# One Exp over four PSUM banks, and a planned fill of the attention steps, in a fused attention and GEGLU kernel

## The chip, the cores and the metric

The kernel runs on one core of one Trainium2 chip. The metric is the device time of one execution in microseconds (us); each kernel is run several times, and the median is compared. TensorE is called PE below, VectorE DVE, ScalarE ACT, GpSimd POOL, and SyncE SP, as the profile has them.

## The reference

One layer norm feeds two branches whose results are added to the input. S = 2048 positions, D = 448 features, H = 16 heads of 28, a sliding window of 256 positions, and F = 1792 hidden features, all bf16.

```python
xn = (x - mean(x)) / sqrt(var(x) + 1e-5)
q, k, v = split(xn @ wqkv)                      # 16 heads of 28
scores = q @ k.T * 28 ** -0.5
mask   = (i - j >= 0) & (i - j < 256)           # causal, 256 wide
a = softmax(where(mask, scores, -1e9)) @ v      # heads joined again
b = (gelu_tanh(xn @ w_gate) * (xn @ w_up)) @ w_down
out = x + a @ wo + b
```

## The kernel before

**Blocks and stages.** The positions are cut into four blocks of 512 (`qb` 0 to 3), each of four tiles of 128. Each block has an attention stage and then a gate stage. Each engine executes its instructions in the order in which the Python code issues them; the order is written out by hand, and engines wait for each other through semaphores.

**Attention stage** (`attention`). The 16 heads are taken in 4 groups of 4 (`g`), and each group in 3 steps (`n`), since a block of 512 queries and its window are cut into three pieces of at most 512 score columns a head. So a block has 12 steps, called steps 0 to 11 here. In a step PE computes the scores `sc` of four heads (keys on the partitions) into four PSUM banks, ACT turns them into `p_sb` with Exp (no maximum is subtracted; a guard at the end checks the sums and branches to a general path that does not run here), and POOL zeroes what lies outside the window (`affine_select`). In the second step of the next group PE multiplies `p_sb` with `v_sb` into `ov` (`pv`); `v_sb` has a column of ones, so that the sums of the softmax come out as one row of `ov`. `ov` is copied to `oc`, the "inverse" chain on DVE (two 32x32 transposes, a small copy, a reciprocal) turns the sums into the factors `rb`, and POOL multiplies `oc` by them into `oN`.

**Fillers.** PE needs other work while ACT does the Exp. Generators deliver it in pieces: `gen_proj` (transposes `tp`, and the projections `pv`, `pq`, `pk` to V, Q and K of the next block), `gen_up` (up projections `ue` done early), and `gen_down` (the output tiles `po` of the block before: 4 matmuls with `wo` on `oN`, 14 with `wd` on `hT`, then DVE adds the input into `res`, and SP stores it). A `Feed` wraps a generator with its estimated time left, and `share` decides after each step's Exp which feed delivers how much; a step that has stopped at `HOLD` does its last matmuls (contraction over the last 64 features, split tiles, "halves") and its copies at the start of the next step. Estimates are in ns of PE time.

**Gate stage** (`gated`). For pairs of 128 hidden features PE computes `gt` and `u`, ACT applies gelu (`ge`), DVE multiplies into `hT`. Gelu and Exp need different ACT tables, so each change of stage loads one. The function `hook` puts statistics of later tiles (`stat`) behind some pairs.

**PSUM.** There are 8 banks: tag `s` 2 x 2 banks (scores, or `gt`), tag `m` two banks, tags `d` and `o` one each. `ov` takes `d` while the current output tile `po` has `o`, and the other way round; `bank` hands out `m` (and `d` in block 0) to the projections in turn.

**Layer norm.** `stat` (DVE), `rstd` (two small ACT operations) and `norm` (DVE) of a tile; before, the four tiles of a later block are scaled in one piece (`prep`) at the beginning of an attention stage, and those of block 1 in the first two steps of block 0.

Of the kernel before, what the change touches and what calls it, by code (L numbers as in the profile page):

```python
# [9 lines left out]
ALU = mybir.AluOpType  # L10
# [6 lines left out]
P = 128  # L17
# [7 lines left out]
HOLD = None  # L25


class Feed:
# [10 lines left out]
    def run(self):  # L39
        self.held = False  # L40
        while self.gens:
# [5 lines left out]
            if c is HOLD:  # L47
                self.held = True
                return 0
# [18 lines left out]


@with_exitstack  # L70
def kernel(
# [18 lines left out]

    xv = A_x.rearrange("b (n p) d -> p (b n) d", p=P)
# [22 lines left out]
    for a in range(2):  # L114
        nc.sync.dma_start(out=wraw[64 * a:64 * a + 64, 3, 0:D], in_=A_wqkv[384:448, a * D:(a + 1) * D])
        nc.sync.dma_start(out=wv[64 * a:64 * a + 64, 3, :], in_=A_wqkv[384:448, 2 * D:3 * D])
# [6 lines left out]
    nc.gpsimd.memset(wo[:, :, :], 0.0)  # L123
# [6 lines left out]
    wo_v = A_wo.rearrange("(g j d) n -> j d g n", g=4, j=4)  # L130
    for j in range(4):
        nc.sync.dma_start(out=wo[32 * j:32 * j + Dh, :, :], in_=wo_v[j])
    nc.sync.dma_start(out=wd[:, :, :], in_=B_w_down.rearrange("(k p) n -> p k n", p=P))

# [20 lines left out]
    def warmup(n):  # L155
        for _ in range(n):
            wps = psum.tile([P, 2, QB], f32, name="wps", tag="s")
            nc.tensor.matmul(wps[:, 0, :], lhsT=warm[:, 0:P], rhs=warm[:, :], start=True, stop=True)
# [14 lines left out]
    def norm(t, eng):  # L173
        xn = work.tile([P, 4, P], bf16, name="xn", bufs=4)
        xf = xn[:, :, :].rearrange("p a b -> p (a b)")
        for lo, n, src in ((0, D, 0), (D, 64, 384)):
            eng.tensor_scalar(out=xf[:, lo:lo + n], in0=x_sb[:, t, src:src + n], scalar1=mv_all[:, t, 0:1],  # L177
                                    scalar2=rstd_all[:, t:t + 1], op0=ALU.subtract, op1=ALU.mult)
        xns[t] = xn

    def prep(qb):
        rstd(4 * qb, 4)
        for t in range(4 * qb, 4 * qb + 4):
            norm(t, nc.vector)
# [30 lines left out]
    def gen_v(qb, ts):  # L215

        for t in ts:
            pvs = []
            for i in range(2):
# [4 lines left out]
                yield 570  # L224
            yield HOLD
# [42 lines left out]
    def gen_down(qb, tags="odod"):  # L268

        hT, oN = hTs[qb], oNs[qb]  # L270
        for tt in range(4):
# [8 lines left out]
            for f in range(NF):  # L280
                nc.tensor.matmul(po[:, 0:D], lhsT=hT[:, f, cs], rhs=wd[:, f, :], start=False, stop=(f == NF - 1),  # L281
                                 skip_group_check=True)
                if f % 4 == 3:
                    yield 755
# [398 lines left out]
```

## Time and profile before

| | before |
|---|---|
| median of 3 runs | 247.76 us (247.2 to 248.15) |
| the profiled execution, its own time | 247.11 us |
| its span, first to last instruction | 245.4 us |
| PE busy | 228.6 us, 93% of the span |
| ACT busy | 141.3 us, 58% |
| DVE busy | 136.9 us, 56% |
| POOL busy | 96.3 us, 39% |
| mean granted PE clock | 0.989 of full speed |

All rows of the trace come from the one profiled execution; its span and its own time differ by what lies around the program. A row of a timeline gives start, length, engine, line, operation, tile written from tiles read, shape, and in brackets how long the engine stood idle before it and which instruction ended that. A row of a group gives busy time and mean ns of one, then idle time before and what ended it. Times of matmuls overlap, so that the distance between starts is the better measure of one.

### The profile page before, as it was taken

Reading aid. Unit: us, or ns where it says so; the run is one execution under the profiler, and the core shown is the slowest. Engines: PE = TensorE matmul, PEld = TensorE weight load, DVE = VectorE, ACT = ScalarE, POOL = GpSimd, SP = SyncE. Lnnn points to the kernel's source line nnn. Section 1 sums busy time; section 2 is a strip of 40 time slices with the busy share of each in tenths; the row PEclk is TensorE's granted clock in tenths of the full one; section 3 lists DMA queues with packets and bytes.
Section 4 is the critical chain, followed back from the end, with each engine's and each line's share of the span. In section 5 each row is a group of like instructions: output and inputs, shape, how many; then the busy total and the mean of one; then the engine's idle time right before and its main releaser. Section 6 shows DMA issues by size and latency. Waiting matters only on the chain.

```text
span 245.4 us, 4264 instructions
## 1 busy us (share of the span) xinstructions
PE 228.6 (93%) x1692; PEld 95.7 (39%) x1712; DVE 136.9 (56%) x272; ACT 141.3 (58%) x169; POOL 96.3 (39%) x120
## 2 busy tenths in 40 slices
PE   7887998999999999999999999999999889999990
PEld 2322432334354434444344334444443334344440
DVE  5977686756662664486663754573321564484311
ACT  3661667753687866633587867643378878645000
POOL 7223275522054865520045765620036677420000
PEclk9997999999999999999999999999999999999998
DMA  7999800000000000000000000000000000000010
GB/s 233 344 300 296 255 7 3 0 1 3 0 19 4 19 3 19 21 0 0 0 23 0 21 0 21 19 0 3 1 19 3 19 0 21 19 0 3 20 40 28
DMA packets 9010, 10.95 MB, mean 45 GB/s; under 512 B 600, under 2 KB 7960, under 8 KB 8984
## 3 DMA queue, kind: packets, MB, share of 16 engines
q1 hardware_dynamic: 8312, 9.69, 13.1%
q10 hardware_dynamic: 672, 0.92, 1.1%
q8 instruction: 15, 0.25, 0.4%
q14 instruction: 11, 0.09, 0.1%
HBM read 8.77 MB, written 1.84 MB: 43 GB/s over the span
## 4 chain that ended last, share of the span: by engine, by line
PE 80%; ACT 8%; DVE 7%; issue 1%; DMA 1%; ACTq 0%
PE po L281 16%; PE gt L197 15%; PE u L197 12%; ACT p_sb L445 7%; PE sc L440 6%; PE gt L202 5%; PE ov L414 5%; PE po L277 4%; PE pk L197 4%; PE pv L197 4%; PE pq L197 3%; PE ue L197 2%; PE pq L202 2%; DVE qT L247 2%; DVE xn L177 1%
## 5 line engine op out<-in xcount | busy, mean ns | idle before, releaser
L451 POOL TENSOR_SCALAR_AFFINE_SELECT p_sb<-p_sb 128x512 bf16<-128x512 bf16 (+1 forms) x92 | 69.5, 777 | 93.8 <-ACT p_sb L445 93.5
L445 ACT ACTIVATE p_sb<-sc 128x1024 bf16<-128x1024 f32 (+2 forms) x96 | 87.9, 969 | 24.5 <-PE sc L440 21.6
L281 PE MATMUL po<-wd,hT 128*128 128x448 bf16 x224 | 49.9, 354 | 0.0
L351 ACT ACTIVATE ge<-gt 128x1024 bf16<-128x1024 f32 x28 | 28.7, 1024 | 34.8 <-PE u L202 22.3
L355 DVE TENSOR_TENSOR hT<-ge,u 128x512 bf16<-128x512 bf16 x44 | 28.1, 679 | 29.4 <-ACT ge L351 29.4
L197 PE MATMUL gt<-xnT,wg 128*128 128x512 bf16 x161 | 39.8, 380 | 0.7 <-issue 0.5
L197 PE MATMUL u<-xnT,wu 128*128 128x512 bf16 x130 | 32.0, 379 | 0.1
L405 POOL TENSOR_TENSOR oN<-oc,rb 128x512 bf16<-128x512 f32 x16 | 20.9, 1305 | 24.6 <-DVE rb L399 24.6
L281 PEld LDWEIGHTS <-hT 128*128 128x128 bf16 x224 | 19.0, 98 | 20.9 <-issue 6.5
L440 PE MATMUL sc<-qT,kT 32*128 32x128 bf16 (+2 forms) x352 | 23.0, 279 | 3.0 <-ACT p_sb L445 2.5
L286 DVE TENSOR_TENSOR res<-po,x_sb 128x448 bf16<-128x448 f32 x16 | 9.7, 608 | 25.5 <-PE po L281 25.5
L197 PEld LDWEIGHTS <-wu 128*128 128x128 bf16 x168 | 16.1, 98 | 20.0 <-issue 1.6
L197 PEld LDWEIGHTS <-wg 128*128 128x128 bf16 x168 | 15.1, 98 | 22.0 <-issue 6.0
L247 DVE CAST qT<-pq 128x512 bf16<-128x512 f32 x16 | 10.9, 682 | 16.1 <-PE pk L202 16.0
L418 ACT COPY oc<-ov 128x512 f32<-128x512 f32 x16 | 9.4, 585 | 16.5 <-PE ov L414 15.3
L197 PE MATMUL pk<-xnT,wkp 128*128 128x512 bf16 x48 | 13.6, 394 | 2.7 <-DVE qT L247 2.7
L277 PE MATMUL po<-wo,oN 128*128 128x448 bf16 x64 | 14.7, 352 | 0.0
L440 PEld LDWEIGHTS <-kT 32*128 32x128 bf16 x352 | 7.6, 92 | 18.3 <-issue 17.3
L202 PE MATMUL gt<-xnT,wgu 64*128 64x512 bf16 x50 | 13.7, 379 | 0.0
L197 PE MATMUL pq<-xnT,wqp 128*128 128x512 bf16 x41 | 13.0, 394 | 0.5 <-issue 0.2
L316 DVE CAST hT<-ue 128x512 bf16<-128x512 f32 x12 | 7.7, 686 | 9.8 <-PE ue L202 9.8
L414 PE MATMUL ov<-p_sb,v_sb 128*32 128x128 bf16 (+2 forms) x352 | 12.8, 277 | 0.0
(65 smaller groups left out, 215.5 us busy)
## 6 DMA issues: line engine op xcount, KB each, us to landing
out_dram<-res SPq DMA_DIRECT2D x16, 112.0 KB, 1.7
wd<-in_B_w_down_dram SPq DMA_DIRECT2D x1, 1568.0 KB, 12.3
wu<-in_B_w_up_dram SPq DMA_DIRECT2D x1, 1344.0 KB
wg<-in_B_w_gate_dram SPq DMA_DIRECT2D x1, 1344.0 KB, 15.1
x_sb<-in_A_x_dram SPq DMA_DIRECT2D x1, 896.0 KB
wraw<-in_A_wqkv_dram ACTq DMA_DIRECT2D x1, 672.0 KB
x_sb<-in_A_x_dram SPq DMA_DIRECT2D x1, 448.0 KB
wo<-in_A_wo_dram SPq DMA_DIRECT2D x4, 98.0 KB
```

The lines of the kernel that those rows point to most:

```text
L197: nc.tensor.matmul(ps, lhsT=lhs(c), rhs=rhs(c), start=start and c == 0, stop=stop and c == 2, skip_group_check=True)
L202: nc.tensor.matmul(ps, lhsT=lhs[p0:p0 + 64], rhs=rhs[p0:p0 + 64], start=start, stop=stop, tile_position=(p0, 0), skip_group_check=True)
L247: nc.vector.tensor_copy(out=qT[:, g, ts], in_=pq[:, :])
L277: nc.tensor.matmul(po[:, 0:D], lhsT=oN[:, g, cs], rhs=wo[:, g, :], start=(g == 0), stop=False, skip_group_check=True)
L281: nc.tensor.matmul(po[:, 0:D], lhsT=hT[:, f, cs], rhs=wd[:, f, :], start=False, stop=(f == NF - 1), skip_group_check=True)
L351: nc.scalar.activation(out=ge[:, :, :], in_=pr["gt"][:, :, :], func=ACT.Gelu_apprx_tanh)
L355: nc.vector.tensor_tensor(out=hT[:, f + i, :], in0=ge[:, i, :], in1=u[:, :], op=ALU.mult)
L405: nc.gpsimd.tensor_tensor(out=oN[:, g, :], in0=oc[:, :], in1=rb[:, :, :].rearrange("p a b -> p (a b)"), op=ALU.mult)
L414: nc.tensor.matmul(ov[32 * j:32 * j + 32, q0:q0 + nq], lhsT=v_sb[:, kt, h, :], rhs=p_sb[:, j, col:col + nq], start=(n == 0 and i == 0), st ...
L440: nc.tensor.matmul(ss[j // 2][:, j % 2, col:col + nq], lhsT=kT[r, g, kt * P:(kt + 1) * P], rhs=qT[r, g, qb * QB + q0:qb * QB + q0 + nq], s ...
L445: nc.scalar.activation(out=p_sb[:, 2 * i:2 * i + 2, 0:ncol], in_=ss[i][:, :, 0:ncol], func=ACT.Exp, scale=SCALE)
L451: nc.gpsimd.affine_select(out=reg, in_=reg, pattern=mid + [[1 if diag else -1, P]], compare_op=ALU.is_ge, fill=0.0, base=0 if diag else -1 ...
```

## The change

- **One Exp a step.** The scores of a step go into one tile of four banks, and one ACT instruction reads them. The pool of that tile has one buffer in attention and is replaced by two buffers of two banks in the gate stage (`score_pool`).
- **`oc` is copied by DVE**, no longer by ACT.
- **`qT` in blocks 0 and 1 is copied by ACT** (`qb > 1` picks DVE), and one V copy more on ACT in block 1.
- **The fill is planned.** `share` gets amounts in ns for the two feeds: what remains, divided by the steps left, less what the step has anyway (`STEP` for scores, `PV` for `ov`), with the second feed's part from a table `plan`. `gen_down` delivers pieces of two matmuls. The last step takes all that is left.
- **Layer norm:** tiles of blocks 2 and 3 are scaled by `hook` in the gate stage before, one tile behind a pair; statistics of tiles 8 to 11 move into the steps of block 0.
- **Block 3** does five pairs' up projections in attention (`early`) instead of four.
- **Start:** the order of the first small weight loads, of two transposes' copies, of `wo`'s memset, and of one V projection.

```diff
-def share(feeds, parts):
-    want = [max(f.left, 0) / n if n else 1e12 for f, n in zip(feeds, parts)]
+def share(feeds, first, second):
+    want = [first, second]
     while True:
-        can = [i for i, f in enumerate(feeds) if f.gens and want[i] > 350 and (parts[i] == 0 or not f.held)]
+        can = [i for i, f in enumerate(feeds) if f.gens and want[i] > 190 and not f.held]
         if not can:
             return
-        i = max(can, key=lambda i: (not feeds[i].held, not feeds[i].closed, min(want[i], feeds[i].left)))
+        i = max(can, key=lambda i: (not feeds[i].closed, want[i]))
...
+def drain(feeds):
+    while any(f.gens for f in feeds):
+        min((f for f in feeds if f.gens), key=lambda f: (f.held, f.closed)).run()
...
+    phase = [None]
+    def score_pool(n):
+        if phase[0] is not None:
+            phase[0].close()
+        phase[0] = ExitStack()
+        phase[0].pool = phase[0].enter_context(tc.tile_pool(name="sps", bufs=n, space=bass.MemoryType.PSUM))
+    score_pool(1)
...
-            nc.vector.tensor_copy(out=qT[:, g, ts], in_=pq[:, :])
+            (nc.vector.tensor_copy if qb > 1 else nc.scalar.copy)(out=qT[:, g, ts], in_=pq[:, :])
             nc.vector.tensor_copy(out=kT[:, g, ts], in_=pk[:, :])
...
-            yield 760
+                if g % 2:
+                    yield 380
             for f in range(NF):
                 nc.tensor.matmul(po[:, 0:D], lhsT=hT[:, f, cs], rhs=wd[:, f, :], start=False, stop=(f == NF - 1),
                                 skip_group_check=True)
-                if f % 4 == 3:
-                    yield 755
+                if f % 2 and f < NF - 1:
+                    yield 375
...
-            nc.scalar.copy(out=oc[:, :], in_=ov[:, :])
+            nc.vector.tensor_copy(out=oc[:, :], in_=ov[:, :])
...
-                ss = [psum.tile([P, 2, QB], f32, name="sc", tag="s") for _ in range(2)]
+                ss = phase[0].pool.tile([P, 4, QB], f32, name="sc", tag="s")
...
-                for i in range(2):
-                    nc.scalar.activation(out=p_sb[:, 2 * i:2 * i + 2, 0:ncol], in_=ss[i][:, :, 0:ncol], func=ACT.Exp, scale=SCALE)
+                nc.scalar.activation(out=p_sb[:, :, 0:ncol], in_=ss[:, :, 0:ncol], func=ACT.Exp, scale=SCALE)
...
-                if qb and left > 10:
-                    share(feeds[:1], (left / 2,))
-                elif not qb and left > 1:
-                    while feeds[0].gens and not feeds[0].held:
-                        feeds[0].run()
-                elif left > 1:
-                    share(feeds, [left + 0.6] + [max(left - 1, 1)] * (len(feeds) - 1))
+                if left == 1:
+                    drain(feeds)
+                elif not qb:
+                    share(feeds + [Feed()], 1e12, 0)
                 else:
-                    share(feeds, [0] * len(feeds))
-                next(aux, None)
+                    to = plan.get(12 - left, 0)
+                    i = 12 - left
+                    whole = sum(f.left for f in feeds) + STEP * left + PV * sum(j > i for j in (4, 7, 10))
+                    ahead = STEP + (PV if n == 0 and g else 0) + (360 if to > 1000 else 0)
+                    share(feeds, whole / (left + 0.2) - ahead - to, to)
+                if aux:
+                    aux.pop(0)()
...
             if qb < 3:
                 feeds.append(Feed((gen_proj(qb + 1), PROJ)))
-                prep(qb + 1)
+                plan = {0: 830, 1: 830, 2: 1140, 4: 1140, 5: 1300, 7: 1300, 8: 1300, 10: 1300}
             else:
                 new_hT(3)
-                early = (2, 6, 8, 10)
+                early = (2, 4, 6, 8, 10)
...
-            elif f >= 4 and qb < 2 and f < 12:
-                stat(4 * qb + 8 + (f - 4) // 2)
+            elif f >= 4 and qb < 2:
+                t = 4 * qb + 4 + f // 2
+                if f < 12:
+                    norm(t + 2)
+                    if qb == 0:
+                        stat(t + 6)
```

The order that results, at the two places on which most hangs. First ACT, at the start of block 0's attention stage. Before, the Exps come in pairs and `lnv`, `rstd_all` (of block 1's layer norm) stand between them:

```order
L229 CAST v_sb<-pv 128x16x28 x3
L445 ACTIVATE p_sb<-sc 128x1024 x2
L168 ACTIVATE lnv<-mv_all,eps_t 128x4
L169 ACTIVATE rstd_all<-lnv 128x4
L445 ACTIVATE p_sb<-sc 128x2x384 x2
```

And after:

```order
L232 CAST v_sb<-pv 128x16x28 x2
L249 CAST qT<-pq 128x512
L447 ACTIVATE p_sb<-sc 128x2048
L177 ACTIVATE lnv<-mv_all,eps_t 128x4
L178 ACTIVATE rstd_all<-lnv 128x4
L249 CAST qT<-pq 128x512
L447 ACTIVATE p_sb<-sc 128x4x384
```

The copies of Q (`qT` from the bank `pq`) now stand on ACT between single Exps. In DVE's queue they stood behind the scaling of two tiles.

Second DVE, in block 3's attention stage, steps 5 and 6. Before (`ue` are the early up projections, `l` to `rb` the inverse chain, `res` a finished output tile):

```order
L316 CAST hT<-ue 128x512 x2
L394 STREAM_TRANSPOSE l_2382<-oc 128x512
L395 COPY l_all<-l_2382 128x16
L397 RECIPROCAL ri<-l_all 128x16
L399 STREAM_TRANSPOSE rb<-ri 128x512
L316 CAST hT<-ue 128x512 x2
```

And after:

```order
L319 CAST hT<-ue 128x512 x2
L397 STREAM_TRANSPOSE l_2316<-oc 128x512
L398 COPY l_all<-l_2316 128x16
L400 RECIPROCAL ri<-l_all 128x16
L402 STREAM_TRANSPOSE rb<-ri 128x512
L319 CAST hT<-ue 128x512 x2
L290 TENSOR_TENSOR res<-po,x_sb 128x448
L421 COPY oc<-ov 128x512
```

A `res` now stands behind the chain and the next two casts, and the copy of `ov`, that was ACT's, behind it. On PE, the rows just ahead of that `ov`, before:

```order
L281 LDWEIGHTS hT
L281 MATMUL po<-wd,hT 128x448
L414 LDWEIGHTS v_sb
L414 MATMUL ov<-p_sb,v_sb 32x128 [waits Pool_49]
L414 LDWEIGHTS v_sb
```

And after, where four matmuls with `wo` stand ahead and, before them, the two that end the tile of the `res` above:

```order
L280 LDWEIGHTS oN
L280 MATMUL po<-wo,oN 128x448
L417 LDWEIGHTS v_sb [waits DVE_49]
L417 MATMUL ov<-p_sb,v_sb 32x128 [waits Pool_49]
L417 LDWEIGHTS v_sb
```

`ov`'s first weight load waits for DVE now, as it did not before.

More of the change, by code (lines that the diff above doesn't have):

```diff
@@ L155, in warmup @@
     def warmup(n):
-        for _ in range(n):
-            wps = psum.tile([P, 2, QB], f32, name="wps", tag="s")
-            nc.tensor.matmul(wps[:, 0, :], lhsT=warm[:, 0:P], rhs=warm[:, :], start=True, stop=True)
+        wps = phase[0].pool.tile([P, 4, QB], f32, name="wps", tag="s")
+        for i in range(n):
+            nc.tensor.matmul(wps[:, i % 4, :], lhsT=warm[:, 0:P], rhs=warm[:, :], start=True, stop=True)
     def stat(t):
```

93 lines of the change are left out of this document (47 added, 46 removed).

## The prediction

> **What bounds the kernel now.** I read the page first, then the busy time per stage, then the timeline of TensorE around its gaps. The page has TensorE (PE) busy for 93% of the span:
>
> ```profile
> PE 228.6 (93%) x1692; PEld 95.7 (39%) x1712; DVE 136.9 (56%) x272; ACT 141.3 (58%) x169; POOL 96.3 (39%) x120
> ```
>
> The number of matmuls does not change, so the change can win only where PE stands still or runs at a lower clock. The four attention stages (blocks 0 to 3) by stage, with PE's busy time as the first number after the length and the granted clock (PEclk) after POOL:
>
> ```profile
> 14.20:46.00 31.80, 27.55 (x215) 10.21 (x216) 22.77 (x44) 19.26 (x29) 15.08 (x20) 0.95 0.52 142
> 66.60:98.90 32.30, 31.70 (x300) 14.10 (x302) 18.03 (x35) 24.56 (x30) 19.56 (x24) 1.00 0.04 12
> 122.50:154.80 32.30, 31.70 (x299) 14.08 (x301) 17.98 (x35) 24.56 (x30) 19.49 (x24) 1.00 0.04 12
> 178.50:208.50 30.00, 28.00 (x265) 11.83 (x269) 11.78 (x21) 24.11 (x27) 19.66 (x24) 1.00 0.04 13
> ```
>
> PE idles 4.25 us in block 0, 0.60 in blocks 1 and 2 each, 2.00 in block 3. Block 0 also loses clock, 0.05 of 31.8 us = 1.6 us. Its largest gap and what lies ahead of it on DVE:
>
> ```profile
> 17.02 0.82 PE L197 MATMUL pq<-xnT,wqp 128*128 128x512 bf16 x3
> 17.15 2.20 DVE L177 TENSOR_SCALAR xn<-x_sb,mv_all,rstd_all 128x448 bf16<-128x448 bf16 x4 [0.69 <-ACT rstd_all L169]
> 19.26 0.68 DVE L247 CAST qT<-pq 128x512 bf16<-128x512 f32 x1
> 19.99 0.81 PE L197 MATMUL pk<-xnT,wkp 128*128 128x512 bf16 x3 [2.15 <-DVE qT L247]
> 20.46 1.11 DVE L177 TENSOR_SCALAR xn<-x_sb,mv_all,rstd_all 128x448 bf16<-128x448 bf16 x4
> ...
> 22.00:23.00 1.00, 1.00 (x4) 0.41 (x3) 0.76 (x2) 0.46 (x1) 0.47 (x1) 0.50 1.05 326
> 25.00:26.00 1.00, 0.95 (x16) 0.77 (x14) 1.00 (x3) 1.00 (x2) 0.00 (x0) 1.00 1.16 256
> ```
>
> The `pk` matmul needs a PSUM bank that the copy `qT` empties, and DVE scales two tiles of the layer norm first. 1.5 us after that gap the clock is at half and PE is busy all the while.
>
> In blocks 1 to 3 the waits are for the Exp. A waiting step shows as two score matmuls, then the other six:
>
> ```profile
> 79.25 0.28 PE L440 MATMUL sc<-qT,kT 32*128 32x256 bf16 x2
> 79.95 0.39 PE L440 MATMUL sc<-qT,kT 32*128 32x256 bf16 x6 [0.42 <-ACT p_sb L445]
> 80.28 0.93 PE L281 MATMUL po<-wd,hT 128*128 128x448 bf16 x4
> ...
> 197.99 0.28 PE L440 MATMUL sc<-qT,kT 32*128 32x256 bf16 x2
> 198.91 0.39 PE L440 MATMUL sc<-qT,kT 32*128 32x256 bf16 x6 [0.63 <-ACT p_sb L445]
> 199.23 0.55 PE L281 MATMUL po<-wd,hT 128*128 128x448 bf16 x2
> ```
>
> Start to start such a step takes 1.03 and 1.24 us, where an unhindered one takes 0.33 (rows below), so 0.70 and 0.91 are lost where the view counts 0.42 and 0.63. Measured so over its 12 steps, block 1 loses 1.45 us, block 2 the same, block 3 3.05.
>
> **The change part by part.** Durations for the sums:
>
> ```profile
> L445 ACT ACTIVATE p_sb<-sc 128x1024 bf16<-128x1024 f32 x80 | 77.5, 1022 | 21.0 <-PE sc L440 18.2 <-POOL p_sb L451 2.7
> L445 ACT ACTIVATE p_sb<-sc 128x512 bf16<-128x512 f32 x8 | 4.3, 594 | 3.5 <-PE sc L440 3.4
> L418 ACT COPY oc<-ov 128x512 f32<-128x512 f32 x16 | 9.4, 585 | 16.5 <-PE ov L414 15.3 <-POOL p_sb L451 1.2
> L247 DVE CAST qT<-pq 128x512 bf16<-128x512 f32 x16 | 10.9, 682 | 16.1 <-PE pk L202 16.0
> L286 DVE TENSOR_TENSOR res<-po,x_sb 128x448 bf16<-128x448 f32 x16 | 9.7, 608 | 25.5 <-PE po L281 25.5
> ...
> 190.30 0.39 PE L202 MATMUL ue<-xnT,wug 64*128 64x512 bf16 x1
> 190.72 1.29 DVE L316 CAST hT<-ue 128x512 bf16<-128x512 f32 x2 [0.54 <-PE ue L202]
> 191.71 1.94 ACT L445 ACTIVATE p_sb<-sc 128x1024 bf16<-128x1024 f32 x2 [0.47 <-PE sc L440]
> 191.93 0.70 DVE L394 STREAM_TRANSPOSE l<-oc 128x512 f32<-128x512 f32 x1
> 193.48 0.71 DVE L399 STREAM_TRANSPOSE rb<-ri 128x512 f32<-128x512 f32 x1
> 193.70 0.39 PE L440 MATMUL sc<-qT,kT 32*128 32x128 bf16 x6 [0.34 <-ACT p_sb L445]
> 195.54 0.84 PE L414 MATMUL ov<-p_sb,v_sb 128*32 128x128 bf16 x24
> 196.31 0.40 PE L440 MATMUL sc<-qT,kT 32*128 32x384 bf16 x8
> 196.64 0.93 PE L281 MATMUL po<-wd,hT 128*128 128x448 bf16 x4
> 232.41 0.92 PE L277 MATMUL po<-wo,oN 128*128 128x448 bf16 x4
> 233.17 2.81 PE L281 MATMUL po<-wd,hT 128*128 128x448 bf16 x14
> 235.82 0.92 PE L277 MATMUL po<-wo,oN 128*128 128x448 bf16 x4
> ```
>
> *One Exp over four banks.* 512 more elements cost 428 ns, so 2048 take 1.022 + 2 x 0.428 = 1.88 us, against 1.94 for the pair: 0.07 less a step. The bounds are 1.88 and two that do not overlap, 2.04; I take 1.88, since the two sizes shown lie on its line. The price is that no score of the next step can start before the whole Exp has ended. A step then cannot be shorter than scores to Exp start (0.42), Exp 1.88, Exp end to scores 0.05: 2.35 us. Before, the limit was little different (Exp pairs at 191.71 and about 2.4 apart), plus 0.585 for the `oc` copy in every third step, which now leaves ACT.
>
> *Equal intervals.* The planned fill of each step in the new order, counted in matmuls: 0.19 us a down matmul (14 from 233.17 to 235.82), 0.77 a `ov` group (195.54 to 196.31), 0.33 the scores, and 0.1 where PE changes between full and split tiles. In blocks 1 and 2 steps 0 to 10 come to 2.3 to 2.8 us, in block 3 to 2.3 to 2.45. Nearly all lie at or just over 2.35. So the waits for the Exp go almost wholly; I leave 0.1 us in a block.
>
> *What is late next, first: step 0.* The table load behind the last gelu holds the first Exp, and the new order puts less work behind the first scores:
>
> ```profile
> 64.63 1.02 ACT L351 ACTIVATE ge<-gt 128x1024 bf16<-128x1024 f32 x1 [0.76 <-PE gt L197]
> 65.67 1.28 ACT L545 ACT_TABLE_LOAD   x1
> 67.41 1.92 ACT L445 ACTIVATE p_sb<-sc 128x1024 bf16<-128x1024 f32 x2
> 69.28 0.49 PE L440 MATMUL sc<-qT,kT 32*128 32x384 bf16 x8
> ```
>
> The Exp can start at the load's end, 66.95, and end at 68.85. Before, step 0 held scores and twelve `wd`, 2.7 us, so it began at 66.6; now it begins two `wo` (0.4) earlier, at 66.2, and holds scores, two `wo`, six `wd` and eight transposes (0.5), 2.4 us: PE is through at 68.6. So 0.3 us is lost in each of blocks 1 to 3, where nothing was lost.
>
> *Second: the attention output by DVE, and `ov`'s bank.* The copy costs DVE between 0.585 and 0.70 us (L418 on ACT, L394 on DVE), I take 0.68 (L247); 16 of them are 10.9 us more for DVE, 9.4 less for ACT. DVE has room on average (18.0 of 32.3 us busy in block 1, 11.8 of 30.0 in block 3) but not in bursts. `ov` takes the bank that `po` of the finished tile held, so its weight load waits until DVE has done `res` (the order shows a wait for DVE there that was absent before). In block 3, step 6: casts of step 4's halves at the start of step 5 (1.3), the inverse chain 191.93 to 194.19 (2.26), the casts of step 5's halves (1.3), then `res` (0.61): with 0.1 to begin, that ends 5.5 us after step 5 began, 3.05 after step 6 began. PE wants `ov` after scores, two `wd` and four `wo`, 1.6 into step 6. So PE waits 1.4 us there, and behind `ov` stand the scores of step 7, for which ACT waits. In step 9 the same reckoning gives 0.25. In blocks 1 and 2 `res` is queued behind an inverse chain in step 6 (0.15) and behind the chain and two casts in step 9 (0.6). All of it is the sum over bursts: at DVE's fastest (each chain 2.0) it falls by half, and with one operation out of the way to nothing.
>
> Blocks 1 and 2: 1.45 before, 0.3 + 0.75 + 0.1 = 1.15 after: 0.3 gained in each. Block 3: 3.05 before, 0.3 + 1.65 + 0.1 = 2.05 after: 1.0 gained.
>
> *Block 0: `qT` by ACT.* ACT copies in 0.585 us what DVE did in 0.68. `pk` no longer stands behind the norms: it waits for the first Exp, the two small rstd operations and one ACT copy, 0.15 us instead of 2.15. What is late next: the second scores for the single Exp (0.45), then `pq` for the `kT` copy, which still stands behind the two norms on DVE (0.3), then the transposes and `pv` (0.35). Of 4.25 us of gaps I leave 1.25. No gap over 0.5 us remains, so I let the half clock go too: 4.25 + 1.6 - 1.25 = 4.6 us gained. The bounds: without the clock's return 3.0; with no wait left 5.9.
>
> [...]
>
> *At nothing:* the norms in the gate stage. Four tiles are 2.2 us of DVE there (1.11 for two, POOL being idle), and a window of block 0's gate has DVE busy 4.67 of 8 us:
>
> ```profile
> 56.00:64.00 8.00, 7.95 (x43) 3.10 (x42) 4.67 (x11) 3.07 (x3) 0.49 (x1) 1.00 0.01 2
> ```
>
> If DVE falls behind, the first transposes of the next block wait for a bank, some 0.1. Also at nothing: statistics of tiles 8 to 11 in block 0's steps (DVE busy 22.8 of 31.8, nothing waits for them but a later rstd); `wo`'s memset behind `wkp`, and the order of the small weight loads (covered until `wo`'s first use in block 1 and by the other weight copies on DVE); five early pairs in place of four in block 3 (eight matmuls of PE only moved); `down` in pieces of two.
>
> Sum: 4.6 + 0.3 + 0.3 + 1.0 = 6.2 us, against the profiled execution's 247.11 us: 240.9. That execution lies 0.65 below the median of the runs, so 241.6 from there; I take **241.3 us**.
>
> **The rivals.**
> - *DVE's bursts cost nothing.* If `res` is always done before `ov`, the 3.15 us of those waits go: 238.1. For it: DVE's mean load. Against: the queue order.
> [...]
> - *The four-bank Exp takes 2.04.* The limit is 2.51, and 33 steps of 2.3 to 2.45 wait some 0.13: 4.3 more, 245.6, so the change would do little of what it says. Against: the slope of the two sizes.
> - *Slower: DVE becomes the bound in attention.* A group of heads needs on DVE `oc` 0.68, chain 2.26, four casts 2.7, and `res` 0.6 to 1.2: 6.2 to 6.8 us of the 7.3 that three steps last. Four norm operations took 2.20 beside a busy POOL and 1.11 beside an idle one (rows above); if such stretching adds over 1.0 a group, DVE sets the pace, and at 0.5 more over 12 groups the gain is gone. At 8.0 us a group, 0.7 x 12 = 8.4 against 6.2: 250. Against: the casts from PSUM keep 0.68 everywhere.
>
> **How the numbers follow.** Forecast 0.53, bursts free 0.20, half clock 0.13, slow Exp 0.07, DVE bound 0.07. The range 237.6 to 245.4 holds the first three. About 0.5% is what a measurement of this kernel can tell from no change (1.2 us). Faster: the first three, 0.86; no change: the slow Exp, 0.07; slower: 0.07.
>
> **What would show it.** Right: one Exp of about 1880 ns a step; no `pk` wait for `qT`; full clock from 21 to 25 us; PE waiting for DVE before `ov` in block 3, over 1 us, and 0.3 before step 1's scores. Wrong: Exp over 2.0; score steps waiting each time; DVE busy over 90% in blocks 1 to 3; a half-clock stretch in block 0.

## The result and the profile after

The changed kernel takes **239.66 us** (median) against 247.48 us of the kernel before on the same chip: a ratio of 0.968, 95% interval 0.963 to 0.973. Run again beside other kernels it took 240.44 us, ratio 0.971 (0.967 to 0.975). The forecast was 241.3 us, range 237.6 to 245.4. The profiled execution took 239.9 us, with a span of 238.2 us against 245.4. One run of the changed kernel (244.5 us, mean clock 0.979), one with four early pairs (245.47, the profiled one, 0.985) and one with the norms ahead (243.33, 0.989) ran at a lower clock, over 1.5% above the fastest of their kernel: the medians hold them, the ratios do not.

The busy times of the page after, and the four attention stages by stage (the columns as in the prediction: length, then PE, PEld, DVE, ACT and POOL busy, granted clock, DMA share, GB/s):

```profile
PE 223.0 (94%) x1690; PEld 94.9 (40%) x1712; DVE 140.5 (59%) x280; ACT 134.8 (57%) x114; POOL 96.7 (41%) x120
```

```profile
15.12:41.70 26.58, 24.80 (x215) 10.02 (x216) 21.88 (x45) 21.25 (x24) 15.36 (x20) 1.00 0.55 156
61.77:93.76 31.99, 31.10 (x300) 13.96 (x303) 18.92 (x36) 24.24 (x16) 20.23 (x25) 1.00 0.04 12
117.01:149.05 32.04, 31.10 (x301) 13.96 (x304) 18.34 (x34) 23.90 (x14) 20.25 (x25) 1.00 0.04 13
172.29:203.00 30.71, 28.87 (x275) 12.64 (x279) 15.58 (x30) 23.52 (x14) 19.84 (x25) 1.00 0.04 12
```

Block 0's attention fell from 31.80 to 26.58 us, at full clock. Block 3's is longer than before (30.71 against 30.0), but it now holds five pairs' up projections instead of four, and its gate stage is shorter by that. So the stages are compared from the end of one gate stage (the first `wo` behind it) to the end of the next, read off the two timelines of PE:

| stretch, us | before | after | gained | predicted |
|---|---|---|---|---|
| start to block 0's first scores | 14.22 | 15.12 | -0.90 | 0 |
| block 0 from there to the end of its gate stage | 51.51 | 46.18 | 5.33 | 4.6 |
| block 1 | 55.91 | 55.23 | 0.68 | 0.3 |
| block 2 | 55.97 | 55.29 | 0.68 | 0.3 |
| block 3, to the tail's first `wo` | 47.79 | 47.10 | 0.69 | 1.0 |
| tail, to the end of the span | 20.00 | 19.28 | 0.72 | 0 |
| sum | 245.40 | 238.20 | 7.20 | 6.2 |

The tail's gain is none of the change: from its first `wo` to the start of its last `wd` group PE needs 11.17 us in both, and from there to the end of the span it took between 8.1 and 8.8 us in the kernels of this study, whatever they changed.

Block 0 after, on PE. Where a copy `qT` on DVE held `pk` back for 2.15 us, five short waits are left, 1.43 us in all:

```profile
17.49 0.34 PE L443 MATMUL sc<-qT,kT 32*128 32x384 bf16 x4 [0.26 <-ACT p_sb L447]
...
19.74 0.29 PE L443 MATMUL sc<-qT,kT 32*128 32x256 bf16 x4 [0.18 <-ACT p_sb L447]
20.43 0.81 PE L201 MATMUL pq<-xnT,wqp 128*128 128x512 bf16 x3 [0.39 <-DVE kT L250]
...
22.79 1.05 PE L196 MATMUL tp<-ident,xn 128*128 128x128 bf16 x16 [0.26 <-DVE kT L250]
24.19 1.31 PE L201 MATMUL pv<-wv,xnT 128*128 128x448 bf16 x6 [0.34 <-DVE xnT L197]
```

The Exp and `oc` by group (busy us, mean ns), and how the Exps follow each other in block 3:

```profile
L447 ACT ACTIVATE p_sb<-sc 128x2048 bf16<-128x2048 f32 x40 | 75.1, 1877 | 24.4 <-PE sc L443 20.3 <-POOL p_sb L453 4.0
L421 DVE COPY oc<-ov 128x512 f32<-128x512 f32 x16 | 11.0, 691 | 21.5 <-PE ov L417 20.1 <-POOL oN L408 1.4
```

```profile
193.55 1.88 ACT L447 ACTIVATE p_sb<-sc 128x2048 bf16<-128x2048 f32 x1 [0.58 <-PE sc L443]
196.00 1.88 ACT L447 ACTIVATE p_sb<-sc 128x2048 bf16<-128x2048 f32 x1 [0.58 <-PE sc L443]
198.46 1.88 ACT L447 ACTIVATE p_sb<-sc 128x2048 bf16<-128x2048 f32 x1 [0.58 <-PE sc L443]
```

The Exp takes the 1.88 us of the forecast, but it repeats every 2.455 us, not every 2.35: the scores of this step start at 195.47 (0.04 after the Exp before has ended) and the Exp at 196.00, 0.53 after them. The 0.42 us that the prediction used came from the kernel before, where the first Exp of a pair waited for half of the scores.

Three waits of PE to which the last sections come back: in step 0 of block 1, before `ov` in its step 9, and at the tail:

```profile
64.47 0.40 PE L443 MATMUL sc<-qT,kT 32*128 32x384 bf16 x8 [0.23 <-ACT p_sb L447]
...
87.54 0.84 PE L417 MATMUL ov<-p_sb,v_sb 128*32 128x128 bf16 x24 [0.34 <-DVE res L290]
...
218.92 0.92 PE L280 MATMUL po<-wo,oN 128*128 128x448 bf16 x4 [0.54 <-DVE hT L358]
```

### The profile page after: what moved, and what is told of

Its sections match the earlier page's. It is cut to its first block, busy times and chain, and to the rows that moved or that the text cites. A ratio compares the mean times of both kernels' runs of the same rounds, so it can differ in the third digit from the quotient of the medians.

```text
span 238.2 us, 4161 instructions
## 1 busy us (share of the span) xinstructions
PE 223.0 (94%) x1690; PEld 94.9 (40%) x1712; DVE 140.5 (59%) x280; ACT 134.8 (57%) x114; POOL 96.7 (41%) x120
## 4 chain that ended last, share of the span: by engine, by line
PE 78%; ACT 10%; DVE 5%; issue 2%; DMA 1%; POOL 1%; SPq 0%; ACTq 0%
PE gt L201 16%; PE po L285 16%; PE u L201 9%; ACT p_sb L447 7%; PE sc L443 6%; PE gt L206 5%; PE ov L417 4%; PE pq L201 4%; PE pv L201 4%; PE pk L201 4%; PE ue L201 3%; PE po L280 3%; DVE xn L186 3%; PE pq L206 2%; ACT ge L354 2%
## 5 line engine op out<-in xcount | busy, mean ns | idle before, releaser
L447 ACT ACTIVATE p_sb<-sc 128x2048 bf16<-128x2048 f32 (+2 forms) x48 | 85.0, 1771 | 26.2 <-PE sc L443 22.0
L358 DVE TENSOR_TENSOR hT<-ge,u 128x512 bf16<-128x512 bf16 x42 | 26.9, 683 | 18.4 <-ACT ge L354 18.3
L201 PE MATMUL u<-xnT,wu 128*128 128x512 bf16 x123 | 30.3, 379 | 0.2
L285 PEld LDWEIGHTS <-hT 128*128 128x128 bf16 x224 | 20.1, 98 | 20.5 <-issue 4.0
L201 PEld LDWEIGHTS <-wg 128*128 128x128 bf16 x168 | 15.1, 98 | 22.0 <-issue 6.0
L421 DVE COPY oc<-ov 128x512 f32<-128x512 f32 x16 | 11.0, 691 | 21.5 <-PE ov L417 20.1
L443 PE MATMUL sc<-qT,kT 32*128 32x128 bf16 (+2 forms) x352 | 18.5, 275 | 1.6 <-ACT p_sb L447 1.3
L280 PE MATMUL po<-wo,oN 128*128 128x448 bf16 x64 | 15.9, 353 | 0.5 <-DVE hT L358 0.5
L319 DVE CAST hT<-ue 128x512 bf16<-128x512 f32 x14 | 9.0, 683 | 11.1 <-PE ue L206 11.1
L201 PE MATMUL pq<-xnT,wqp 128*128 128x512 bf16 x39 | 12.1, 380 | 1.2 <-issue 0.5
L186 DVE TENSOR_SCALAR xn<-x_sb,mv_all,rstd_all 128x448 bf16<-128x448 bf16 (+1 forms) x32 | 12.1, 428 | 0.8 <-ACT rstd_all L178 0.8
```

The source lines that it names most:

```text
L201: nc.tensor.matmul(ps, lhsT=lhs(c), rhs=rhs(c), start=start and c == 0, stop=stop and c == 2, skip_group_check=True)
L280: nc.tensor.matmul(po[:, 0:D], lhsT=oN[:, g, cs], rhs=wo[:, g, :], start=(g == 0), stop=False, skip_group_check=True)
L358: nc.vector.tensor_tensor(out=hT[:, f + i, :], in0=ge[:, i, :], in1=u[:, :], op=ALU.mult)
L443: nc.tensor.matmul(ss[:, j, col:col + nq], lhsT=kT[r, g, kt * P:(kt + 1) * P], rhs=qT[r, g, qb * QB + q0:qb * QB + q0 + nq], start=True, s ...
L447: nc.scalar.activation(out=p_sb[:, :, 0:ncol], in_=ss[:, :, 0:ncol], func=ACT.Exp, scale=SCALE)
```

## The experiments

The start of a program turned out to vary, and so did the times. The stretch from block 0's first scores to the tail's first `wo` does not: it took 203.80, 203.80 and 203.81 us in three executions of the same order of work (the changed kernel twice, and with one memset moved). It is called the main stretch below, and small effects are read from it.

| kernel | median, us | ratio to before (95%) | first scores at | main stretch |
|---|---|---|---|---|
| before | 247.2 to 247.5 | | 14.22 | 211.18 |
| changed | 239.66 | 0.968 (0.963 to 0.973) | 15.12 | 203.80 |
| changed, again | 240.44 | 0.971 (0.967 to 0.975) | 15.40 | 203.80 |
| `qT` by DVE | 245.19 | 0.988 (0.983 to 0.993) | 16.95 | 208.65 |
| `oc` by ACT | 242.55 | 0.981 (0.975 to 0.988) | 14.85 | 205.42 |
| two Exps | 241.48 | 0.975 (0.970 to 0.980) | 14.03 | 205.34 |
| memset early | 239.48 | 0.968 (0.964 to 0.972) | 14.04 | 203.81 |
| before, `qT` by ACT | 242.92 | 0.983 (0.978 to 0.987) | 14.21 | 206.76 |
| four early pairs | 242.24 | 0.978 (0.972 to 0.984) | 17.49 | 206.91 |
| flat plan | 250.36 | 1.012 (1.006 to 1.018) | 15.09 | 213.85 |
| two tiles | 241.19 | 0.976 (0.972 to 0.981) | 15.24 | 204.48 |
| inverse behind `res` | 240.05 | 0.970 (0.964 to 0.976) | 16.14 | 203.31 |
| norms ahead | 241.68 | 0.968 (0.964 to 0.973) | 16.99 | 204.10 |
| six pairs, memset early | 237.70 | 0.959 (0.957 to 0.962) | 14.42 | 202.10 |

### Block 0: the copy `qT`, undone and alone

```diff
-            (nc.vector.tensor_copy if qb > 1 else nc.scalar.copy)(out=qT[:, g, ts], in_=pq[:, :])
+            nc.vector.tensor_copy(out=qT[:, g, ts], in_=pq[:, :])
```

> Edit: in the changed kernel the copy qT goes back to DVE in blocks 0 and 1 too; nothing else. Mine (block 0 stands still for DVE's queue: norms, then qT): a wait of PE of 1.5 to 2.2 us for DVE qT near 20 us appears again, and the clock drops to half behind it; block 0's attention (first scores to gate) grows from 26.6 us by 2 (gap alone) to 4 us (gap and half clock), the time is 242 to 244 us. If the gap comes back and the clock stays full, the clock loss was not the gap's. Rival (block 0 was won by the one Exp and by the pieces without HOLD, the place of qT does little): no wait over 0.5 us, at most 0.5 us lost, 239.4 to 240.4 us.

The same edit the other way round, in the kernel before:

> Edit: the kernel before, with one part of the change alone: qT is copied by ACT in blocks 0 and 1. Mine (the wait for qT behind two norms and the half clock behind it were nearly all of block 0's loss; its return cost 4.85 us of stage time in the changed kernel): block 0's attention falls from 31.8 us to 27 to 28 us, no half clock in it, the time is 242.6 to 243.9 us. Rival (the gain needs the new order of the pieces, the one Exp and the place of the norms besides): under 2 us gained, 245.4 us or more.

Undone, block 0's attention took 31.43 us (4.85 more), with the wait back and the half clock behind it. PE's timeline, then slices of 1 us (granted clock third from the end), of the kernel with `qT` by DVE:

```profile
19.60 0.82 PE L201 MATMUL pq<-xnT,wqp 128*128 128x512 bf16 x3
22.57 0.81 PE L201 MATMUL pk<-xnT,wkp 128*128 128x512 bf16 x3 [2.15 <-DVE qT L249]
...
23.85 1.38 PE L201 MATMUL pq<-xnT,wqp 128*128 128x512 bf16 x3
```

```profile
22.00:23.00 1.00, 0.43 (x3) 0.19 (x2) 1.00 (x2) 0.00 (x0) 0.48 (x1) 1.00 1.01 387
23.00:24.00 1.00, 1.00 (x9) 0.31 (x8) 1.00 (x5) 0.03 (x1) 0.00 (x0) 0.98 1.10 216
24.00:25.00 1.00, 1.00 (x3) 0.29 (x2) 1.00 (x3) 0.99 (x1) 0.00 (x0) 0.50 1.11 226
...
27.00:28.00 1.00, 1.00 (x20) 0.64 (x18) 0.92 (x2) 0.39 (x1) 0.00 (x0) 0.81 1.10 284
```

Alone, in the kernel before, it took block 0's attention to 27.37 us at full clock:

```profile
14.21:41.58 27.37, 25.99 (x215) 10.22 (x217) 18.86 (x37) 22.39 (x36) 15.24 (x20) 1.00 0.66 162
```

So one copy on another engine is worth 4.4 to 4.85 us of the 7.38 by which the main stretch fell. (The median of 245.19 lies above the range given: the profiled execution started 1.8 us later than the changed kernel's, which the section on the start takes up.) The clock followed the gap in both traces that have it: 1.4 to 1.5 us behind the wait's end it fell to half for 3.4 us, and three matmuls 128x512 took 1.38 us instead of 0.82. None of the other twelve traces, which lack this wait, shows a half clock in block 0. So the loss of 1.6 us that the prediction took from one row came with the wait and went with it. It did not come in every execution, though: 25 runs of the kernel before are listed with their mean clock, and four of them have 0.998, where this stretch alone (1.7 of 245 us) would leave 0.993 at most. These four took 246.38 to 246.74 us, where the medians are 247.2 to 247.5.

### `oc` by ACT again

```diff
-            nc.vector.tensor_copy(out=oc[:, :], in_=ov[:, :])
+            nc.scalar.copy(out=oc[:, :], in_=ov[:, :])
```

> Edit: oc is copied by ACT again, as before the change; nothing else. Mine now (the copy runs beside the next step's scores: 0.585 us against 0.42 us from ov's end to the Exp's start, so it holds each Exp of a second step back by 0.17 us, 12 to 16 times, 2 to 2.7 us at most and less where the step has slack; DVE gets 0.69 us of room in each group and gives back up to 0.8 us before ov in block 3 and 0.3 in each of blocks 1 and 2): 239.5 to 241.5 us. Rival (the whole 0.585 us stands in the chain of Exps, as the prediction put it): 12 x 0.585 = 7 us of waits of PE for the Exp less 1.4: 245 us. Other rival (DVE's bursts are what is left to win): under 239 us.

The main stretch grew by 1.62 us: the copy on DVE is a gain, far from the rival's 5 us. (The profiled run, 241.31 us, lies in the range given; two runs without a trace took 243.8 us and put the median a microsecond above it, for which no cause is shown.) DVE's room gave nothing back. With `oc` off DVE, `ov` waits in block 3's step 6 as long as before (0.82 us in the changed kernel):

```profile
190.49 0.84 PE L417 MATMUL ov<-p_sb,v_sb 128*32 128x128 bf16 x24 [0.89 <-DVE res L290]
```

That part of my expectation, and the prediction's "with one operation out of the way to nothing", is wrong.

### What stands ahead of `res`

In the changed kernel, DVE and PE around that step of block 3:

```profile
186.09 0.70 DVE L397 STREAM_TRANSPOSE l<-oc 128x512 f32<-128x512 f32 x1
...
187.32 0.71 DVE L402 STREAM_TRANSPOSE rb<-ri 128x512 f32<-128x512 f32 x1
187.96 1.25 DVE L319 CAST hT<-ue 128x512 bf16<-128x512 f32 x2
189.13 0.61 DVE L290 TENSOR_TENSOR res<-po,x_sb 128x448 bf16<-128x448 f32 x1
```

```profile
188.05 0.92 PE L280 MATMUL po<-wo,oN 128*128 128x448 bf16 x4
189.79 0.84 PE L417 MATMUL ov<-p_sb,v_sb 128*32 128x128 bf16 x24 [0.82 <-POOL oN L408]
```

The row names POOL's `oN`, which ended in the same moment as `res`. The edit moves the chain of the transposes behind the step's pieces:

```diff
-                inverse()
                 if n == 1 and g:
...
+                if n == 0 or left == 1:
+                    inverse()
                 if aux:
```

> Edit: the inverse chain of a group (two transposes, a copy, a reciprocal on DVE) is issued behind the pieces of step 0 of the next group instead of at the start of the step behind ov's copy, so that it stands behind res in DVE's queue; nothing else. Mine (ov in block 3's step 6 waits for res, and res stands behind the chain's 1.94 us and two casts): the wait of 0.82 us falls to 0.2 to 0.3, block 3 takes 30.1 to 30.3 us instead of 30.71; step 9 of blocks 1 and 2 is unchanged, since res waits there for the last wd of its own tile; 0.5 us in all, at the edge of what times can tell. Rival (the wait is for POOL's oN, as the row names it, and for the copy oc on DVE): no change, 30.7 us.

```profile
173.31:203.54 30.23, 28.88 (x276) 12.63 (x279) 15.16 (x26) 23.52 (x14) 19.28 (x24) 1.00 0.04 12
```

```profile
190.33 0.84 PE L417 MATMUL ov<-p_sb,v_sb 128*32 128x128 bf16 x24 [0.34 <-DVE res L290]
```

Block 3 takes 30.23 us instead of 30.71, the wait is 0.34, and blocks 1 and 2 are as they were. So `ov` waits for `res`, and the inverse chain's 1.94 us ahead of it in DVE's queue make 0.48 of the 0.82 us of that wait; the name `oN` in the row was the last of two that came together. For the 0.34 us that are left `res` still stands behind the step's two casts, as the prediction's sum had it too. The time (240.05 us) says nothing of 0.5 us.

### One Exp: split on one tile, and on two

```diff
-                nc.scalar.activation(out=p_sb[:, :, 0:ncol], in_=ss[:, :, 0:ncol], func=ACT.Exp, scale=SCALE)
+                for i in range(2):
+                    nc.scalar.activation(out=p_sb[:, 2 * i:2 * i + 2, 0:ncol], in_=ss[:, 2 * i:2 * i + 2, 0:ncol], ...)
```

> Edit: the Exp of a step is split again in two instructions over two banks each; both halves read one four-bank tile, so the next scores still wait for the second half. Nothing else. Mine (the pair takes 1.94 to 1.95 us against 1.877, and nearly all steps are filled by PE to 2.44 to 2.62 us, above the floor of 2.42 us that results): +0 to +0.8 us, 240 to 240.7 us, hardly more PE waits for p_sb. Rival (the Exps are the chain that sets the pace): +0.07 us in each of 48 steps, 3.4 us, 243.3 us.

```diff
-                ss = phase[0].pool.tile([P, 4, QB], f32, name="sc", tag="s")
+                ss = [phase[0].pool.tile([P, 2, QB], f32, name="sc", tag="s") for _ in range(2)]
...
-                        nc.tensor.matmul(ss[:, j, col:col + nq], ...
+                        nc.tensor.matmul(ss[j // 2][:, j % 2, col:col + nq], ...
```

> Edit: the scores lie again in two tiles of two banks with an Exp each, as before the change; all else as in the changed kernel. Rival (the one Exp is what was won): 0.07 us more in each of the 23 to 33 steps that run at the Exp's period, 1.6 to 2.3 us slower than the changed kernel, 241.5 us. Mine (a pair on tiles of its own repeats in 2.41 us in the kernel before, since scores of the next step begin in the first tile while the second Exp runs, where the single Exp repeats in 2.455): blocks 1 to 3 0 to 0.5 us shorter each, 238.7 to 239.9 us: the one Exp has won nothing, the equal filling and the copies on other engines have.

Block 3's attention of the one and of the other, each followed by the Exp pairs of two full steps:

```profile
172.26:203.45 31.19, 29.58 (x279) 12.94 (x279) 15.69 (x30) 24.19 (x26) 19.75 (x25) 1.00 0.04 12
```

```profile
193.82 1.94 ACT L448 ACTIVATE p_sb<-sc 128x1024 bf16<-128x1024 f32 x2 [0.58 <-PE sc L443]
196.33 1.94 ACT L448 ACTIVATE p_sb<-sc 128x1024 bf16<-128x1024 f32 x2 [0.58 <-PE sc L443]
```

```profile
172.99:203.81 30.82, 29.33 (x276) 12.70 (x280) 15.58 (x30) 24.23 (x26) 19.72 (x25) 1.00 0.04 12
```

```profile
194.29 1.94 ACT L448 ACTIVATE p_sb<-sc 128x1024 bf16<-128x1024 f32 x2 [0.49 <-PE sc L443]
196.75 1.94 ACT L448 ACTIVATE p_sb<-sc 128x1024 bf16<-128x1024 f32 x2 [0.52 <-PE sc L443]
```

On one tile the pair costs 0.48 us in block 3, 0.05 us a step: there the Exps set the pace, as the rival said, and "hardly more waits" was wrong. Over the main stretch it is 1.54 us, half of the rival's 3.4. On two tiles the cost is 0.11 us in block 3, 0.13 in blocks 1 and 2 each, 0.3 at the start of block 0's gate stage: 0.68 in all. Both expectations miss that number, mine by its sign. In full steps the pair on one tile repeats every 2.51 us, the pair on two tiles every 2.46, the single Exp every 2.455: there the one Exp wins nothing over the two of before. So the title of the change, one Exp in place of two, is worth 0.7 us of the main stretch: the saved instructions bring 1.54, and the tile of four banks by itself, which makes all scores wait for the whole Exp, costs 0.86 of that (205.34 less 204.48).

### The plan and the early pairs

```diff
-                plan = {0: 830, 1: 830, 2: 1140, 4: 1140, 5: 1300, 7: 1300, 8: 1300, 10: 1300}
+                plan = {i: PROJ / 11 for i in range(11)}
...
-                plan = {1: 1300, 4: 1300, 5: 1300, 7: 1300, 10: 1300}
+                plan = {i: UP1 * len(early) / 11 for i in range(11)}
```

> Edit: the plan's numbers are replaced by one equal share for each of the steps 0 to 10 (blocks 1, 2: 1027 ns; block 3: 755 ns); nothing else. By counts of matmuls the steps of blocks 1 and 2 then hold 2.15, 2.69, 2.69, 2.71, 2.70, 2.70, 2.71, 1.09, 1.09, 1.48, 2.23 us and the last 6.0, those of block 3 2.12 and 2.44 in turn. Mine (each step waits for what it lacks to 2.455 us): 3.4 us more in each of blocks 1 and 2, 0.7 us in block 3, 7.5 us slower than the changed kernel, 247 us. Rival (the waits for the Exp are small whatever the filling, since PE has work between, and what counts is the work in all): within 1 us of the changed kernel, 239.5 to 240.7 us.

Three short steps of block 1 with this plan, each with its wait:

```profile
84.64 0.40 PE L443 MATMUL sc<-qT,kT 32*128 32x256 bf16 x8 [1.20 <-ACT p_sb L447]
...
87.09 0.40 PE L443 MATMUL sc<-qT,kT 32*128 32x128 bf16 x8 [1.19 <-ACT p_sb L447]
...
89.55 0.40 PE L443 MATMUL sc<-qT,kT 32*128 32x384 bf16 x8 [0.80 <-ACT p_sb L447]
```

These steps start 2.45 us apart, though they hold 1.1 to 1.5 us of work by the counts. The attention of block 1 grew by 4.50 us, of block 2 by 5.07, of block 3 by 1.11: more than the 3.4, 3.4 and 0.7 of the count, since pieces that stand close together also wait for DVE's copies (`pq` 1.1 us for `qT`, 0.8 for `v_sb`, in both blocks together). In block 2 the clock fell to half at the end of the second of these gaps (1.20 and 1.19 us; the eight scores behind it took 0.62 us instead of 0.40, and the clock over the block's attention was 0.95); in block 1 the same gaps did not do it (1.00):

```profile
61.75:98.24 36.49, 31.66 (x301) 14.54 (x304) 19.66 (x37) 24.95 (x16) 22.13 (x27) 1.00 0.03 11
121.27:158.38 37.11, 32.98 (x301) 14.64 (x304) 19.09 (x35) 24.61 (x14) 22.13 (x27) 0.95 0.03 11
```

The smaller edit of the same kind:

```diff
-                early = (2, 4, 6, 8, 10)
+                early = (2, 6, 8, 10)
```

> Edit: block 3 computes four up pairs early (2, 6, 8, 10) in place of five, in the changed kernel; the numbers of the plan stay. What is moved is eight matmuls from attention to gate. As the prediction had it (only moved, at nothing): block 3 from its first scores to the tail's first wo unchanged within 0.3 us, 239.4 to 240 us; with the tail's wait for hT gone 0.5 less. Mine now (a step whose filling is shorter than the period of the Exp, 2.455 us, waits for the rest: by counts of matmuls the eleven steps of block 3 lack 1.9 us in the changed kernel and 5.1 us here, since the gate gets the work that the steps lack): 3.1 us slower, 242.5 to 243 us.

The main stretch grew by 3.11 us, the number expected, but from other parts. A step that was left almost empty made PE wait 1.57 us, and the clock was at half for 3.4 us behind it (slices of 1 us again):

```profile
201.91 0.49 PE L443 MATMUL sc<-qT,kT 32*128 32x256 bf16 x8 [1.57 <-ACT p_sb L447]
```

```profile
202.00:203.00 1.00, 1.00 (x10) 0.31 (x9) 0.22 (x1) 0.48 (x1) 1.00 (x2) 0.55 0.00 0
203.00:204.00 1.00, 1.00 (x4) 0.46 (x3) 0.63 (x1) 1.00 (x1) 0.62 (x1) 0.50 0.00 0
...
205.00:206.00 1.00, 1.00 (x6) 0.45 (x5) 0.00 (x0) 0.70 (x1) 1.00 (x3) 0.75 0.14 47
```

By the clock of these slices that is 1.7 us of the 3.11. The waits before `ov` (0.8) and for `hT` at the tail (0.54) went, so that by subtraction the waits for the Exp cost 2.75 more. These rows are of the execution of 245.47 us. Two others, of 240.78 and 241.28 us, had mean clocks of 0.997 and 0.998 and so no such half clock (1.7 of 239 us). The fifth pair, which the prediction priced at nothing, is thus worth 1.4 us in the main stretch by subtraction, and 3.1 where the half clock comes too.

### The norms in the gate stage

```diff
-                    norm(t + 2)
...
                 feeds.append(Feed((gen_proj(qb + 1), PROJ)))
+                for t in range(4 * qb + 4, 4 * qb + 8):
+                    norm(t)
```

> Edit: the layer norm of the next block's four tiles is issued ahead of the attention of blocks 1 and 2 again, as before the change, not in the gate stage of the block before; nothing else. As the prediction had the move (at nothing in the gate; it did not price what it saves): the norms then hold DVE for 2.2 to 4.4 us from the block's start, and the plan has the first eight transposes in step 0, so PE waits for them: 0.5 to 1.2 us more in each of blocks 1 and 2, 1 to 2.4 us in all. Rival (the first step waits for the table load of the Exp anyway, which covers them): at most 0.3 us in a block.

Block 1's attention grew from 31.99 to 32.22 us, block 2's from 32.04 to 32.11: the rival is right, and the move is worth 0.3 us. The time (241.68 us, beside 240.44 of the changed kernel) can't tell 0.3 us; in the trace the first scores came late, at 16.99 us (next section).

### The start

> Edit: the memset of wo on POOL stands again ahead of the copies wkp, as before the change; the order of the weight loads stays new. Nothing else. Mine (the 0.9 us by which block 0's first scores start later come from DVE's layer norm of tile 2 and 3 running beside POOL's memset: four operations took 2.19 us instead of 1.31): first scores at 14.2 to 14.6 us instead of 15.12, 239.0 to 239.4 us. Rival (POOL's wkp copies, which now start at 6.02 us instead of 8.87, slow the norms, wherever the memset stands): first scores still at 15.0 us, time unchanged, 239.5 to 240.1 us.

```diff
     nc.gpsimd.memset(v_sb[:, :, :, Dh + 1:32], 0.0)
+    nc.gpsimd.memset(wo[:, :, :], 0.0)
...
-    nc.gpsimd.memset(wo[:, :, :], 0.0)
     nc.vector.tensor_copy(out=w3p[:, :, 0:Dh], ...
```

> No edit: the changed kernel once more, to stand beside the others on the same chip, and to see whether its start varies. Mine (block 0's first scores come at 14.0 to 17.5 us by whether POOL's copies and its memset fall beside DVE's norms; the stages after that repeat within 0.05 us): block 0 26.6, block 1 32.0, block 2 32.0, block 3 30.7 us again, runs that lie 2 us or more apart, median 239.5 to 241. Rival (the start of 15.12 us is fixed by the order of POOL's queue): 15.1 us again, runs within 1 us.

DVE's norms, POOL, and what PE waits for, in the changed kernel; then the norms of the same two tiles with the memset early:

```profile
6.02 1.63 POOL L502 COPY wkp<-wraw 128x448 bf16<-128x448 bf16 x3 [2.37 <-DMA wraw<-in_A_wqkv_dram]
7.60 1.59 POOL L503 MEMSET wo<- 128x1792 bf16 x1
...
7.84 2.19 DVE L186 TENSOR_SCALAR xn<-x_sb,mv_all,rstd_all 128x448 bf16<-128x448 bf16 x4
...
9.37 0.43 PE L196 MATMUL tp<-ident,xn 128*128 128x128 bf16 x4 [1.47 <-DVE xn L186]
```

```profile
7.58 1.36 DVE L187 TENSOR_SCALAR xn<-x_sb,mv_all,rstd_all 128x448 bf16<-128x448 bf16 x4
```

With the memset early the first scores came at 14.04 us, and the main stretch is unchanged. But the start varies: the same late memset gave 14.03 us in one kernel (two Exps) and 15.1 to 17.5 in most. POOL's copies start when the weights `wraw` land, between 6.0 and 8.9 us in the traces of this study, and the memset follows; whether they fall beside DVE's norms differs from execution to execution. With the late memset the four norms of tiles 2 and 3 took 1.57 to 2.69 us in five traces, and the first three of them alone 1.98 to 3.32 us in three others; with the early one all four took 1.29 to 1.36 us in three traces, `wkp`'s copies beside them or not. In the kernel with four early pairs the half clock came too: PE waited 1.97 us for the norms, the clock was 0.50 in the slices from 11 to 14 us, six matmuls `pv` took 2.44 us instead of 1.30, and the first scores came at 17.49. In ten profiled executions with the late memset the first scores came at 14.03 to 17.49 us (median 15.3), in four with the early one (two of them with the whole start of the kernel before) at 14.04 to 14.42. So the late memset can hold the norms back. What else moves the first scores, such as the time at which the inputs land, is not separated. The medians of two studies, 239.48 against 239.66 and 240.44, don't separate the edit alone, since six runs of the changed kernel lie 1.9 us apart.

Beside POOL's `wkp` and memset the norms from SBUF to SBUF took 2.19 us for four (rows above), against 1.11 beside an idle POOL (kernel before, block 0, at 20.46 us), while the copy `qT` from PSUM took 0.68 us beside POOL's mask there (at 19.26 us). Why a norm takes longer beside POOL is not shown.

### A faster version

```diff
-                early = (2, 4, 6, 8, 10)
+                early = (2, 4, 6, 8, 10, 12)
...
-                plan = {1: 1300, 4: 1300, 5: 1300, 7: 1300, 10: 1300}
+                plan = {1: 1300, 2: 1300, 4: 1300, 5: 1300, 7: 1300, 8: 1300}
```

and the memset early.

> Edit, a version meant to beat both: the changed kernel with the memset of wo ahead of the copies wkp, six early up pairs in block 3 (2 to 12) in place of five, and the plan of block 3 set to 1300 in steps 1, 2, 4, 5, 7, 8, so that no ov follows within a step on the tile whose bank it takes. Mine (each step waits for what its filling lacks to 2.455 us: the eleven steps of block 3 lack 1.2 us instead of 1.9; the 0.8 us of waiting for DVE res before ov in step 6 goes too): block 3 from its first scores to the tail's first wo 45.1 to 45.7 us instead of 46.63, first scores of block 0 at 14.0 to 14.3 us instead of 15.1, 237.3 to 238.3 us. Rival (casts of a sixth pair load DVE in block 3, and its bursts are what PE waits for): 46.6 us or more in block 3, 239 us.

```profile
171.58:203.03 31.45, 31.01 (x284) 13.17 (x288) 18.06 (x33) 24.11 (x14) 20.43 (x26) 1.00 0.04 12
```

It takes 237.7 us (237.14 to 238.28), 2.7 less than the changed kernel beside it, and the two intervals do not touch. Of the 2.7 us the main stretch holds 1.70; the rest lies at the start and the end. Block 3 from its first scores to the tail's first `wo` takes 44.94 us instead of 46.63, a little better than expected: PE is busy for 31.01 of 31.45 us, `ov` in step 6 waits for nothing, and the tail's wait for `hT` is gone. The sixth pair's casts cost nothing (DVE is busy 18.06 us of 31.45).

## Why the prediction was right, and where its steps were not

- **Block 0, 4.6 us forecast, 5.33 measured.** The mechanism stands: undone and alone, the copy gives 4.85 and 4.4 us. The residual waits are the ones named, 1.43 us for 1.25: 0.44 for the Exp (in two steps, 0.26 and 0.18) for 0.45, 0.39 for `kT` ahead of `pq` for 0.3, and 0.60 before the transposes and `pv` for 0.35; `pk`'s 0.15 did not come. What 5.33 has over the copy's 4.4 are parts to which the prediction gave nothing in this block: with `oc` back on ACT it took 0.63 us longer, with two tiles of scores 0.30. That the full clock would come back was right: with the wait of 2.15 us gone, the clock of block 0's attention was 1.00 instead of 0.95.
- **The step's floor, 2.35 us: failed.** It is 2.455, since one Exp over four banks waits for all eight scores (0.53 us), not half of them (0.42). So the waits for the Exp did not go "almost wholly". A filling of 2.23 to 2.32 us (by counts of matmuls, block 3 after) lacks 0.13 to 0.22 in each of the first eleven steps, 1.9 us in all by this estimate, where the prediction left 0.1.
- **The waits before `ov`, 3.15 us: too large, for the right reason.** 0.82 us in block 3's step 6 instead of 1.4, 0.34 in step 9 of blocks 1 and 2 instead of 0.6, none in their step 6 instead of 0.15 nor in step 9 of block 3 instead of 0.25: 1.50 us in all. The inverse chain took 1.94 us, not 2.26. What the prediction blamed on `oc` was not `oc`'s: the copy on DVE is a gain of 1.6 us. In block 3 this error and the one before cancelled: 0.69 gained for 1.0.
- **Step 0's wait of 0.3 us: right**, 0.23, 0.28 and 0.35 us in blocks 1 to 3.
- **At nothing.** Right for the norms (0.3 us if put back). Wrong for the memset behind `wkp`: the start was 0.9 us longer in this execution, up to 3 in others, though not by the memset alone. Wrong for the fifth pair, which fills steps that would wait (1.4 us, 3.1 with a half clock), and which brought a wait of 0.54 us for DVE's last `hT` at the tail.
- **The rivals.** Of "bursts free" more than half came true, and it gave 238.1; "DVE becomes the bound" did not happen (59% busy), nor did the half clock, given 0.13, in block 0 (clock 1.00). The four-bank Exp took 1.877 us on average, not 2.04.

The sum missed by 1.0 us in the profiled execution (7.20 for 6.2) with errors of both signs. That the start's 0.90 us lost and the tail's 0.72 gained nearly cancel, neither of which it had, is luck. Not settled: what the plan alone gave. Undoing `qT`, `oc` and the one Exp (two tiles) costs 4.85, 1.62 and 0.68 us, which makes 7.15 of the 7.38 us of the main stretch, but the parts need not add up, and the old rule of sharing was not run with the new pieces.

## What to carry to other kernels

Fill each step to the measured period of its slowest chain, counted from release to release (here 2.455 us: Exp, hand-over, and all scores that it needs), and not to the duration of the instruction; what a step lacked was lost here although PE was 94% busy (with four early pairs the waits for the Exp cost 2.75 us more, by subtraction). Look first for one copy in the wrong queue: a wait of 2.15 us cost 4.4 to 4.85 here, in part because the clock followed. When times scatter by more than the effect, compare a stretch that repeats (0.01 us here) instead of the whole.

## What the runs showed of the hardware

- Half clock behind short waits, and not each time: a wait of 2.15 us had it behind it in the traces of both kernels with that wait (before, and `qT` by DVE), 1.57 us in block 3 of the kernel with four early pairs had it, two of 1.2 us, 2.45 us apart, had it in block 2 of the flat plan and not in block 1. At the start 1.97 us with four early pairs had it, and 1.47 us with `qT` by DVE (six matmuls `pv` 2.43 us instead of 1.30); 1.47 us in the changed kernel did not, nor did 1.68 us with the inverse behind `res` and 1.69 us with the norms ahead. By their mean clock (0.998) four of 25 runs of the kernel before were without the stretch that 2.15 us brought in the trace. In the slices the half clock lasted 3.4 us each time (kernel before, `qT` by DVE, four early pairs at the start and in block 3).
- A small copy on DVE from SBUF to SBUF (128x16) took 1.03 us beside POOL's mask, in the kernel with the chain behind `res`, where it took 0.17 beside an idle POOL in the changed kernel (at 186.82 us):

```profile
190.92 1.03 DVE L398 COPY l_all<-l 128x16 f32<-128x16 f32 x1
```

```profile
190.82 1.69 POOL L452 TENSOR_SCALAR_AFFINE_SELECT p_sb<-p_sb 128x1024 bf16<-128x1024 bf16 x2 [1.31 <-ACT p_sb L446]
```
